# Who writes the order of three engines' queues: a scheduler or the program itself, in a two-layer attention and MLP kernel

## The chip, the core and the metric

The kernel runs on one core of one Trainium2 chip. The core has four engines that compute, each with a queue of its own that it works through in order: TensorE (PE in the profile, with PEld for the loading of its stationary operand), VectorE (DVE), ScalarE (ACT) and GpSimd (POOL). SyncE (SP) issues most of the DMAs here, ScalarE a few. Matmuls write PSUM, which has eight banks of 2 KB per partition; everything else lies in SBUF. The metric is the time of one execution on the device in microseconds, as the median of several runs.

## What is computed

Two layers of attention with a sliding window and an MLP, both with residuals and with the same weights in both layers. In short:

```
H, Dh, W = 32, 20, 256                       # S = 2048 rows, D = 640, F = 1536
def A(x):                                    # x already normalized
    q, k, v = split(x @ wqkv)                # heads of 20
    s = q k^T * Dh**-0.5, kept where 0 <= i - j < W
    return softmax(s) v @ wo
def B(x):
    h = relu(x @ w1 + b1)
    return (h * h) @ w2 + b2
for _ in range(2):
    x = x + A(layernorm(x))
    x = x + B(layernorm(x))
```

Input and output are float32. The dense products are made of three float16 products each, high by high, high by low and low by high part (`mm3`), so every operand of a dense matmul is written twice: a cast gives the high part, and a subtraction gives the low part.

## The kernel before

**Units.** The 2048 rows are cut into eight groups of 256 for each layer, so there are `NU = 16` units; unit `u` is group `u % 8` of layer `u // 8`. A unit's keys are its own 256 rows and those of the unit before. Weights stay in SBUF after the first 200 us or so, in which they are loaded and split.

**Attention of a unit.** `stage_qk` and `stage_v` make q, k and v with dense matmuls (line 155, as all of them). The two halves of q and k (tile `qd`: ScalarE writes the high part at L251, VectorE the low part at L252, from the PSUM tile `acc`) go out to DRAM and come back spread over partitions (`spread`). The 32 heads are worked in eight quads. For each quad there are three parts. `max_quad` makes the scores with rows as partitions (L321, 18 matmuls of a normal unit), and VectorE adds the mask and takes the row maximum in eight reductions (L335). `exp_quad` makes the scores again with keys as partitions (L371, 16 matmuls), with the maximum folded into the product as two more rows of `qt`; ScalarE takes six exponentials (L378), and GpSimd sets to zero what the window excludes, in eight instructions (L389, L393). `pv_quad` multiplies by V (L418, 32 matmuls in four columns of the array), with a column of ones that gives the sum of each row; ScalarE copies the result out (L428), and every second quad goes to DRAM.

**The rest of a unit.** `load_o` loads the attention's output and its row sums (`rs`) back, with the rows that the residual needs. `norm_o` divides: one reciprocal of all of `rs` (L464), two products (L467), two casts (L469) and two subtractions (L470), by halves of 128 columns. `stage_o` is the output projection with the residual (L482) and the second layer norm; `y_cross` and `ln_cross` cast and subtract the normalized rows (L220, L221) and transpose them by DMA (`cross`), while `stage_y` and `ln_t` transpose on TensorE. `stage_f` is the MLP: w1, then for each 128 hidden features relu (L517), square on GpSimd (L520), cast (L521) and subtraction (L522), then w2 and the residual (L534). `add_b2` adds the last bias on GpSimd (L492) to the residual rows.

**Order on TensorE.** It is the order of the program (`manual_schedule` for PE). `together` deals the eight quads of unit `u` out in turns: the exponential scores of one quad, a share of dense work, the maximum scores of a quad `LEAD = 5` quads ahead, pv, and dense work again. The dense work is a chain of generators: in a normal unit `stage_qk(u+1)`, `stage_o(u-1)`, `y_cross`, `stage_v(u+1)` and `stage_f(u-1)`.

**Order on the other engines.** It comes from the framework's scheduler, which replays the program on a timeline of its own and takes priorities: `first()` raises the priority of an instruction that reads a dense PSUM tile. The division of unit `u-1` is placed in the program by a `hook` in `stage_qk` (L242) between two tiles of k. The scheduler may move it.

**Buffers that tie engines together.** All dense products, pv and the small transposes share two PSUM banks (tag `mm`, `bufs=2`): a new tile waits until the tile two before it has been read. The scores share the other six (`bb`: three banks per half of the heads, `bufs=2`, taken in pairs), so the exponential scores wait for the reductions before them, and the maximum scores for the exponentials. The exponentials' output `pt` has six buffers, relu's output `r` two, `qd` one. `apart` declares that a matmul into one bank of `bb` doesn't depend on reads of the others, so that reads and matmuls of one quad may overlap.

Of the kernel before, what the change touches and what calls it, by code (L numbers as in the profile page):

```python
# [42 lines left out]
def kernel(ctx: ExitStack, tc: tile.TileContext, x, wqkv, wo, w1, b1, w2, b2, out):  # L43
# [47 lines left out]

    wq_s = sb.tile([P, 2, KC, 3 * D], F16, name="wq_s")
# [70 lines left out]
    def layernorm(src, y):  # L163

        st = sb.tile([P, 2, 6], F32, name="bst", bufs=2)
        for i in range(2):
            nc.vector.bn_stats(st[:, i, :], src[:, i * HD:(i + 1) * HD])
        mv = sb.tile([P, 4], F32, name="bmv", bufs=2)
        nc.vector.bn_aggr(mv[:, 0:2], st)
        nc.vector.tensor_scalar(mv[:, 2:3], mv[:, 1:2], 1e-5, YS ** -2, op0=ALU.add, op1=ALU.mult)  # L170
        power = nc.gpsimd.tensor_tensor(mv[:, 3:4], mv[:, 2:3], neghalf, op=ALU.pow)
        return nc.vector.tensor_scalar(y, src, mv[:, 0:1], mv[:, 3:4], op0=ALU.subtract, op1=ALU.mult), power

    def split_t(y, dst):

        for c0, n in ((0, 3), (3, 2)):
            tr = ps.tile([P, 4, P], F32, name="tr", tag="mm", bufs=2)
            for c in range(n):
                nc.tensor.transpose(tr[:, c, :], y[:, (c0 + c) * P:(c0 + c + 1) * P], ident)
            with first():  # L180
                nc.scalar.copy(dst[:, 0, c0:c0 + n], tr[:, :n])
                nc.vector.tensor_sub(dst[:, 1, c0:c0 + n], tr[:, :n], dst[:, 0, c0:c0 + n])  # L182
            yield 117 * n

# [11 lines left out]
    def ln_load(u):  # L196
# [3 lines left out]
        for i in range(2):  # L200
            xt = sb.tile([P, D], F32, name="xt", tag="xt", bufs=2)
            nc.sync.dma_start(xt, xsrc(l, 2 * g + i))
            did = layernorm(xt, xt)
            ys.append(xt)
            if u == 0:
                norm[:] = did
# [3 lines left out]
    def ln_t(u):  # L210
        ys = lns.pop(u)
        yTs[u] = yT = sb.tile([P, 2, KC, T], F16, name="yT", tag="yT", bufs=1)
        for i in range(2):
            yield from split_t(ys[i], yT[:, :, :, i * P:(i + 1) * P])

    def cross(ys, dst, tag):

        yl = sb.tile([P, 2, 2, D], F16, name="yl", tag=tag, bufs=1)
        for i, y in enumerate(ys):
            nc.scalar.copy(yl[:, i, 0], y)  # L220
            nc.vector.tensor_sub(yl[:, i, 1], y, yl[:, i, 0])  # L221
            for a in range(2):
                nc.sync.dma_start_transpose(dst[:, a, :, i * P:(i + 1) * P], yl[:, i, a])

    def ln_cross(u):

        ln_load(u)
        yTs[u] = sb.tile([P, 2, KC, T], F16, name="yT", tag="yT", bufs=1)
        cross(lns.pop(u), yTs[u], "qd")

    held = []

    def stage_qk(u, hold=False, hook=None):
# [4 lines left out]
        for j, dst in enumerate((qt, kt)):  # L238
            qd = sb.tile([P, KC, 2, T], F16, name="qd", tag="qd", bufs=1)
            for c0 in range(0, KC, 2):  # L240
                n = min(2, KC - c0)
                if hook and j and c0 == 2:  # L242
                    hook()
                acc = ps.tile([P, 2, T], F32, name="acc", tag="mm", bufs=2)
# [5 lines left out]
                with first():  # L250
                    at[0] = nc.scalar.activation(qd[:, c0:c0 + n, 0, :], acc[:, :n, :], AF.Copy, scale=s)  # L251
                    nc.vector.scalar_tensor_tensor(qd[:, c0:c0 + n, 1, :], acc[:, :n, :], s, qd[:, c0:c0 + n, 0, :],  # L252
                                                   op0=ALU.mult, op1=ALU.subtract)

            dr = tc.dram_tile([D, 3, T], F16, name=f"qk{u}_{j}")
            drv = dr.rearrange("(c p) t n -> p c t n", p=P)
            nc.sync.dma_start(drv[:, :, j:j + 2, :].rearrange("p c t n -> p c (t n)"),
                              qd.rearrange("p c a n -> p c (a n)"))
            nc.sync.dma_start(drv[:, :, 2 - 2 * j, :], qd[:, :, 0, :])
            if hold and j == 0:  # L260
                held.append((dst, dr))
            else:
                spread(dst, dr)
# [6 lines left out]
    def stage_v(u):  # L270
        yT = yTs.pop(u)
        for i in range(2):
            vt = vts[(2 * u + i) % 6][0]
            for h in range(2):
                acc = ps.tile([P, 2, T], F32, name="acc", tag="mm", bufs=2).rearrange("p a n -> p (a n)")
                yield from mm3(acc[:, :HD], lambda a, k: yT[:, a, k, i * P:(i + 1) * P],
                               lambda b, k: wq_s[:, b, k, 2 * D + h * HD:2 * D + (h + 1) * HD], KC, 136)
                with first():
                    at[0] = nc.scalar.activation(vt[:, h * NP:(h + 1) * NP, 0:DH],
                                                 acc[:, :HD].rearrange("p (h d) -> p h d", d=DH),  # L280
                                                 AF.Copy, scale=1.0 / (YS * WS))

# [3 lines left out]

    def banks():
        return [ps.tile([P, 3, 512], F32, name="bb", tag="bb", bufs=2) for e in range(2)]

    def apart(ins, others):  # L290

        for it in others:
            tc.declare_no_dep(ins.ins, it.ins, reason="other banks")

    def max_quad(n):
# [10 lines left out]

        found, read = [], []
        for w in (3, 0, 1, 2):
# [5 lines left out]
            o = parts[0][3]  # L314
            if w == 3:
                parts = [(kt, z, z + P, c + z - a) for kt, a, b, c in parts for z in range(a, b, P)]
            for kt, a, b, c in parts:
                for e in range(2):
                    r = slice(64 * e, 64 * e + 3 * DH)
                    to = bb[e][:, c // P, 3 * P:] if w == 3 else bb[e][:, w, c:c + b - a]  # L320
                    apart(nc.tensor.matmul(to, qt[r, p, i * P:(i + 1) * P], kt[r, p, a:b], start=True, stop=True),  # L321
                          read)
            now = []
            for e in range(2):
                s0 = p % (2 * GQ)
                accum = mx[:, e, s0, i:i + 1]
                if w == 3:
                    now.append((bb[e][:, o // P:, 3 * P:], maskb[:, o:].rearrange("p (a n) -> p a n", n=P), accum))
                else:
                    now.append((bb[e][:, w, o:3 * P], maskb[:, o:], accum))  # L330
            if w == 3:
                found = now
                continue
            for v, mask, accum in now + (found if w == 2 else []):
# [369 lines left out]
```

## Time and profile before

| | us |
|---|---|
| median of 3 runs | 1806.36 (1806.29 to 1808.37) |
| profiled execution | 1805.37 |
| its span, first to last instruction | 1803.6 |
| TensorE busy | 1632.8 (91% of the span) |
| VectorE busy | 975.7 (54%) |
| ScalarE busy | 760.7 (42%) |
| GpSimd busy | 631.2 (35%) |
| mean granted TensorE clock | 0.965 of full speed |

How to read the profile's lines: in a group of instructions, the line of the kernel, engine, operation, output<-input by the program's names, shapes and count come first; behind the first bar the busy time in us and the mean of one in ns; behind the second bar the time that the engine idled just before these instructions, and what ended that idle time. In a timeline, the first two numbers are start and duration in us, and the square bracket holds the idle time before and what ended it. In a table of stretches each row has the stretch, its length, the busy time of PE, PEld, DVE, ACT and POOL with their counts, the granted clock, the busy share of the DMA engines and GB/s.

### The profile page before, as it was taken

Reading aid. Unit: us, or ns where it says so; the run is one execution under the profiler, and the core shown is the slowest. Engines: PE = TensorE matmul, PEld = TensorE weight load, DVE = VectorE, ACT = ScalarE, POOL = GpSimd, SP = SyncE. Lnnn points to the kernel's source line nnn. Section 1 sums busy time; section 2 is a strip of 40 time slices with the busy share of each in tenths; the row PEclk is TensorE's granted clock in tenths of the full one; section 3 lists DMA queues with packets and bytes.
Section 4 is the critical chain, followed back from the end, with each engine's and each line's share of the span. In section 5 each row is a group of like instructions: output and inputs, shape, how many; then the busy total and the mean of one; then the engine's idle time right before and its main releaser. Section 6 shows DMA issues by size and latency. Waiting matters only on the chain. (4 is left out here: it accounts for less than half of the span.)

```text
span 1803.6 us, 44320 instructions
## 1 busy us (share of the span) xinstructions
PE 1632.8 (91%) x17542; PEld 1185.7 (66%) x17542; DVE 975.7 (54%) x3041; ACT 760.7 (42%) x1620; POOL 631.2 (35%) x1306
## 2 busy tenths in 40 slices
PE   4667699999999999999999999999999999898889
PEld 3444476766767676676777666676766767675567
DVE  6344555565565556556446565555656565555331
ACT  4355253533435343353534244353533435343522
POOL 4244152523425242342513243342423324242512
PEclk9888899999999999999999999999999999998999
DMA  5573303325152332515243342514234251331110
GB/s 180 143 189 97 96 10 106 79 71 133 39 132 54 100 85 71 133 35 132 58 121 71 97 100 71 129 34 126 55 89 111 60 126 46 95 73 38 35 54 20
DMA packets 230344, 157.42 MB, mean 87 GB/s; under 512 B 79608, under 2 KB 211064, under 8 KB 230136
## 3 DMA queue, kind: packets, MB, share of 16 engines
q1 hardware_dynamic: 221792, 145.08, 32.1%
q10 hardware_dynamic: 8344, 9.51, 1.8%
q8 instruction: 138, 2.26, 0.5%
q14 instruction: 70, 0.57, 0.1%
HBM read 84.68 MB, written 52.95 MB: 76 GB/s over the span
## 5 line engine op out<-in xcount | busy, mean ns | idle before, releaser
L335 DVE CUSTOM_DVE_ANT_0 bb<-bb,maskb 128x384 f32<-128x384 f32 (+2 forms) x1024 | 512.2, 563 | 129.3 <-PE bb L321 112.4
L378 ACT ACTIVATE pt<-bb 128x512 f32<-128x512 f32 x736 | 370.5, 603 | 224.5 <-PE bb L371 224.2
L389 POOL TENSOR_SCALAR_AFFINE_SELECT pt<-pt 128x256 f32<-128x256 f32 x448 | 186.2, 421 | 627.5 <-ACT pt L378 615.5
L155 PE MATMUL acc<-y,w_s 128*128 128x256 f16 x2880 | 333.5, 275 | 2.4 <-DVE y L182 2.2
L155 PE MATMUL acc<-w_s,hh 128*128 128x320 f16 x2304 | 327.6, 300 | 0.2
L155 PEld LDWEIGHTS <-w_s 128*128 128x128 f16 x2880 | 278.5, 99 | 59.1 <-issue 24.0
L155 PE MATMUL acc<-yT,wq_s 128*128 128x256 f16 x2400 | 296.4, 285 | 9.7 <-DVE qd L252 5.3
L155 PEld LDWEIGHTS <-hh 128*128 128x128 f16 x2304 | 222.4, 98 | 99.0 <-issue 15.9
L155 PEld LDWEIGHTS <-wq_s 128*128 128x128 f16 x2400 | 239.0, 102 | 69.5 <-issue 33.5
L418 PE MATMUL pv<-pt,vt 128*32 128x128 f32 (+1 forms) x3840 | 204.5, 344 | 56.3 <-DVE qd L252 36.6
L393 POOL TENSOR_SCALAR_AFFINE_SELECT pt<-pt 128x256 f32<-128x256 f32 x512 | 206.8, 427 | 60.3 <-ACT pt L378 59.3
L428 ACT COPY ot<-pv 128x256 f32<-128x256 f32 x128 | 47.5, 371 | 376.4 <-PE pv L418 376.4
L418 PEld LDWEIGHTS pv<-pt,vt 128*32 128x32 f32 x3840 | 111.3, 113 | 110.0 <-issue 61.3
L522 DVE TENSOR_TENSOR hh<-r,hh 128x256 f16<-128x256 f32 x192 | 84.2, 449 | 181.1 <-ACT hh L521 174.8
L155 PE MATMUL acc<-wo_s,od 128*128 128x320 f16 x960 | 141.3, 301 | 25.1 <-ACT od L469 9.8
L520 POOL TENSOR_TENSOR r<-r 128x256 f32<-128x256 f32 x192 | 116.5, 627 | 130.7 <-ACT r L517 130.7
L155 PE MATMUL acc<-wq_s,yT 128*128 128x320 f16 x960 | 142.1, 301 | 6.3 <-DVE qd L252 3.3
L335 DVE DVE_READ_ACCUMULATOR2_ANT mx<- 128x1 f32 x1024 | 145.0, 142 | 0.0
L155 PEld LDWEIGHTS <-od 128*128 128x128 f16 x960 | 91.7, 98 | 72.1 <-issue 27.2
L252 DVE SCALAR_TENSOR_TENSOR qd<-acc,qd 128x512 f16<-128x512 f32 (+1 forms) x96 | 56.4, 598 | 140.9 <-ACT qd L251 140.9
L371 PE MATMUL bb<-qt,kt 62*128 62x128 f16 (+1 forms) x1920 | 110.8, 246 | 22.5 <-DVE mx L335 18.0
L155 PEld LDWEIGHTS <-yT 128*128 128x128 f16 x960 | 93.1, 99 | 50.4 <-issue 15.5
(63 smaller groups left out, 1150.0 us busy)
## 6 DMA issues: line engine op xcount, KB each, us to landing
qk<-qd SPq DMA_DIRECT2D x32, 640.0 KB
qt<-qk SPq DMA_DIRECT2D x32, 480.0 KB
kt<-qk SPq DMA_DIRECT2D x32, 480.0 KB
o<-ot SPq DMA_DIRECT2D x256, 42.0 KB
qk<-qd SPq DMA_DIRECT2D x32, 320.0 KB
od<-o SPq DMA_DIRECT2D x14, 640.0 KB
stg<-in_B_w_dram ACTq DMA_DIRECT2D x30, 256.0 KB
xt<-in_A_x_dram SPq DMA_DIRECT2D x16, 320.0 KB
```

The lines of the kernel that those rows point to most:

```text
L155: nc.tensor.matmul(acc, lhs(a, c), rhs(b, c), start=(k == 0), stop=(k == 3 * nk - 1))
L252: nc.vector.scalar_tensor_tensor(qd[:, c0:c0 + n, 1, :], acc[:, :n, :], s, qd[:, c0:c0 + n, 0, :], op0=ALU.mult, op1=ALU.subtract)
L335: read.append(nc.vector.tensor_tensor_reduce(out=v, in0=v, in1=mask, scale=1.0, scalar=-3.0e38, op0=ALU.add, op1=ALU.max, accum_out=accum))
L371: apart(nc.tensor.matmul(bb[e][:, k, o:o + w], kt[r, 2 * qd + j, ko:ko + P], qt[r, 2 * qd + j, q0 * P:q0 * P + w], start=True, stop=True), ...
L378: at[0] = nc.scalar.activation(pt[:, :o], bb[e][:, k, :o], AF.Exp, scale=SCALE / (QS * QS))
L389: nc.gpsimd.affine_select(out=m, in_=m, pattern=[[0, 2], [-1, P]], compare_op=ALU.is_gt, fill=0.0, base=0, channel_multiplier=1)
L393: nc.gpsimd.affine_select(out=m, in_=m, pattern=[[0, 2], [1, P]], compare_op=ALU.is_ge, fill=0.0, base=0, channel_multiplier=-1)
L418: nc.tensor.matmul(pv[32 * jj:32 * (jj + 1), q0 * P:(q0 + qn) * P], vf[:, c:c + 32], pj[:, j, :], start=(k == 0), stop=(k == len(steps) - ...
L428: nc.scalar.copy(ot[:, qd % 2], pv)
L520: nc.gpsimd.tensor_tensor(r, r, r, op=ALU.mult)
L522: nc.vector.tensor_sub(hh[:, 1, f0 + f, :], r, hh[:, 0, f0 + f, :])
```

## The change

ScalarE, VectorE and GpSimd get the order of the program from unit 1 on (`manual_schedule` for the three). So that the program's order is a useful one, the instructions are no longer written where they arise, but posted as jobs. A job has an engine, a cost in ns, a function that writes the instruction, jobs it depends on, an earliest time and a priority (0 for what frees a PSUM tile of the dense work, 1 for exponentials, masks and reductions, 2 for what has time). A small clock runs along with the program: every piece of dense work adds its ns (`step`), each score and pv block a constant, and after each step `pump` puts down the jobs whose start on their engine's clock is no more than 250 ns ahead. `need` puts a job down at once, with what it depends on, where TensorE's next instruction needs it. Units before 1 put each job down at once and leave the order to the scheduler as before.

The following goes with it:

- The division is posted by `load_o` itself in four quarters of 64 columns, each a reciprocal, a product, a cast and a subtraction, with an earliest time 7 us later; `norm_o` and the hook are gone. The first layer norm and `add_b2` get earliest times of 4 us, and `add_b2` is cut into four halves of 320 columns.
- In `max_quad` all 18 matmuls are written before the eight reductions, and in `exp_quad` all 16 before the six exponentials. `apart` is gone.
- `y_cross` and `ln_cross` post their casts and subtractions; DMAs that follow a job are issued when the job is put down.
- TensorE's instructions stand in the same order, but for four matmuls near the end (`upto(dense, 10e3)` in place of 6e3 and 4e3).

The core of the diff:

```diff
+    now, clk, pend, ordered = [0.0], {"A": 0.0, "D": 0.0, "G": 0.0}, [], [False]
+    LOOK, LAT = 250.0, 80.0
+    class Job:
+        def __init__(self, eng, cost, fn, deps, nb, prio):
...
+        def start(self):
+            return max([clk[self.eng], self.nb] + [d.end + LAT for d in self.deps])
+        def put(self):
+            t = self.start()
+            self.out = self.fn()
+            self.end = clk[self.eng] = t + self.cost
+    def post(eng, cost, fn, *deps, wait=0.0, prio=1):
+        j = Job(eng, cost, fn, [d for d in deps if d is not None], now[0] + wait, prio)
+        if ordered[0]:
+            k = len(pend)
+            while k and pend[k - 1].prio > prio:
+                k -= 1
+            pend.insert(k, j)
...
+    def pump():
...
+            for j in pend:
+                if all(d.end is not None for d in j.deps) and j.start() <= now[0] + LOOK:
+                    pend.remove(j)
+                    j.put()
...
+    def need(*js):
+        for j in js:
+            if j.end is None:
+                need(*j.deps)
+                pend.remove(j)
+                j.put()
+            now[0] = max(now[0], j.end)
+    def step(ns):
+        now[0] += ns
+        pump()
+    def mm_tile(shape, name):
+        while len(banks2) > 1:
+            need(*banks2.pop(0))
+        t = ps.tile(shape, F32, name=name, tag="mm", bufs=2)
+        banks2.append([])
+        return t, banks2[-1]
...
     def stage_qk(u, hold=False):
-                if hook and j and c0 == 2:
-                    hook()
+                lo_ = post("D", 60 + 265 * n, low, post("A", 60 + 225 * n, high, prio=0), prio=0)
+                jobs.append(lo_)
+            need_later(lo_, lambda j=j, dst=dst, qd=qd: leave(u, j, dst, qd, hold))
...
     def banks():
+        need(*bbjobs)
+        bbjobs.clear()
         return [ps.tile([P, 3, 512], F32, name="bb", tag="bb", bufs=2) for e in range(2)]
...
+                bbjobs.append(post("D", 115 + 1.04 * (3 * P - o), lambda v=v, mask=mask, accum=accum:
+                                   nc.vector.tensor_tensor_reduce(...)))
...
+                ex = post("A", 30 + 0.9 * o, power)
+                bbjobs.append(ex)
...
+                    masks.append(post("G", 410, mask, ex))
...
     def load_o(u, late=False):
+        for i in range(4):
+            q = slice(i * T // 4, (i + 1) * T // 4)
...
+            j = post("D", 460, ratio, wait=7e3, prio=2)
+            j = post("D", 400, times, j, prio=2)
+            j = post("A", 350, high, j, prio=2)
+            js.append(post("D", 400, low, j, prio=2))
-    def norm_o(u):
...
     def add_b2(u, *after):
+            for h in range(2):
+                js.append(post("G", 870, lambda x1=x1s[u, i], hs=hs:
+                               nc.gpsimd.tensor_tensor(x1[:, hs], x1[:, hs], box["b"][:, hs], op=ALU.add),
+                               wait=4e3, prio=2))
...
     def stage_f(u, ahead=None):
+                j = post("A", 380, relu, *hj[f0 + f - 2:f0 + f - 1], prio=0)
+                jobs.append(j)
+                j = post("G", 630, square, j, prio=0)
+                j = post("A", 330, high, j, prio=0)
+                hj.append(post("D", 430, low, j, prio=0))
...
+        if u == 1:
+            ctx.enter_context(tc.manual_schedule(engines={mybir.EngineType.Activation, mybir.EngineType.DVE,
+                                                          mybir.EngineType.Pool}))
+            ordered[0] = True
```

351 lines of the change are left out of this document (219 added, 132 removed).

## The prediction

> **What bounds the kernel now.** I read the page first, then the busy time by stage, then the idle time of TensorE by what ended it, and last one unit in order of time. A unit is 256 rows of one layer, some 105 us; it has eight turns, each with the scores of one quad for the exponential (tile bb, L371), the scores of a later quad for the row maximum (bb, L321), the product with V (pv, L418), and dense matmuls (L155) between.
>
> ```profile
> PE 1632.8 (91%) x17542; PEld 1185.7 (66%) x17542; DVE 975.7 (54%) x3041; ACT 760.7 (42%) x1620; POOL 631.2 (35%) x1306
> 0.00:200.00 200.00, 127.60 (x1051) 87.01 (x1051) 91.02 (x324) 93.37 (x194) 76.21 (x106) 0.86 0.57 156
> 200.00:300.00 100.00, 91.09 (x1043) 63.74 (x1044) 58.95 (x187) 42.70 (x91) 35.55 (x80) 0.94 0.11 33
> 300.00:1600.00 1300.00, 1235.15 (x13660) 905.66 (x13659) 751.16 (x2323) 551.39 (x1171) 451.81 (x979) 0.98 0.37 89
> ```
>
> TensorE is the bound. Its instruction order is the same in the changed kernel but for four matmuls of the tail, so only its idle time and its clock can move. Of 170.8 us idle, 72.4 lie in the first 200 us, where the order hardly changes. From 300 to 1600 us it idles 64.9 us. Who ends that idle time, in the groups by line of this stretch:
>
> ```profile
> L418 PE MATMUL pv<-pt,vt 128*32 128x256 f32 (+1 forms) x3040 | 160.0, 345 | 48.4 <-DVE qd L252 33.9 <-POOL pt L393 11.2 <-ACT r L517 3.3
> L155 PE MATMUL acc<-wo_s,od 128*128 128x320 f16 x780 | 112.7, 299 | 9.7 <-DVE qd L252 9.7
> L371 PE MATMUL bb<-qt,kt 62*128 62x256 f16 (+1 forms) x1536 | 85.7, 244 | 5.8 <-DVE bmv L169 2.5 <-DVE mx L335 1.5 <-DVE bmv L170 1.4
> ```
>
> Three quarters of it hangs on one instruction, VectorE's low half of qd (L252), because pv needs the PSUM bank that it frees. One unit on VectorE and TensorE shows why it is late:
>
> ```profile
> 394.93 1.75 DVE L464 RECIPROCAL rs<-rs 128x256 f32<-128x256 f32 x1 [3.09 <-DMA rs<-o]
> 397.00 1.56 DVE L467 TENSOR_TENSOR od<-od,rs 128x640 f32<-128x640 f32 x2 [0.32 <-DMA od<-o]
> 398.62 1.56 DVE L470 TENSOR_TENSOR od<-od 128x640 f16<-128x640 f32 x2
> 400.10 0.68 DVE L252 SCALAR_TENSOR_TENSOR qd<-acc,qd 128x512 f16<-128x512 f32 x1
> 400.93 2.79 PE L418 MATMUL pv<-pt,vt 128*32 128x256 f32 x32 [2.51 <-DVE qd L252]
> 407.72 0.83 PE L371 MATMUL bb<-qt,kt 62*128 62x256 f16 x16
> 414.27 1.51 PE L418 MATMUL pv<-pt,vt 128*32 128x256 f32 x32
> 418.87 2.20 PE L155 MATMUL acc<-wo_s,od 128*128 128x320 f16 x15 [0.81 <-DVE qd L252]
> 442.86 0.99 PE L418 MATMUL pv<-pt,vt 128*32 128x256 f32 x8 [1.76 <-POOL pt L393]
> 456.23 4.00 PE L155 MATMUL acc<-y,w_s 128*128 128x256 f16 x35
> ```
>
> VectorE stands 3.09 us at the reciprocal for a DMA, does the whole division, and only then qd; TensorE idles 2.51 us. The gap also costs clock: the same 32 pv matmuls take 2.79 us behind it and 1.51 us at 414.27. The stretches of these two, with the granted clock as third from last:
>
> ```profile
> 400.93:403.70 2.77, 2.77 (x33) 1.56 (x34) 2.77 (x11) 0.00 (x0) 0.00 (x0) 0.50 0.00 0
> 414.27:415.78 1.51, 1.51 (x37) 0.93 (x34) 1.51 (x7) 0.00 (x0) 0.00 (x0) 1.00 1.08 217
> ```
>
> **The change, part by part.** *Division in quarters, 7 us after its load (load_o).* In the built order the eight maximum reductions and qd's low half now stand ahead of the first quarter. The maximum scores of this turn end at 398.4 (400.93 less the wait), the reductions 4.2 us later (below), so the first quarter comes no sooner than 402.6, when the DMA of 394.93 has long landed. Both waits go: -33.9 us, and -2.28 for the same wait at 295.04 (below).
>
> ```profile
> 295.04 2.79 PE L418 MATMUL pv<-pt,vt 128*32 128x256 f32 x32 [2.28 <-DVE qd L252]
> 1552.80 2.79 PE L418 MATMUL pv<-pt,vt 128*32 128x256 f32 x32 [4.10 <-DVE qd L252]
> 1650.26 1.75 DVE L464 RECIPROCAL rs<-rs 128x256 f32<-128x256 f32 x1 [7.97 <-DMA rs<-o]
> 1648.43 2.35 PE L155 MATMUL acc<-w_s,hh 128*128 128x320 f16 x16
> 1658.90 1.95 PE L371 MATMUL bb<-qt,kt 62*128 62x256 f16 x16 [8.12 <-DVE mx L335]
> ```
>
> The clock: eight such pv, these two the first and the last of them, at 2.79 for 1.51: 8 x 1.28 = 10.2 us; the other units' gaps cool less or not at all. With the exponential scores at 1658.90 (1.95 for 0.83) I take -11.3 us.
> The Trainium skill, "TensorE: Matmul & The Clock Gate", Part 1, says that the clock drops after at least one idle window of about 3.4 us. By that a gap of 2.5 us costs no clock, and of this term only the two gaps over 3.4 us (4.10 and 8.12) would remain, 2.4 us; the trace disagrees (clock 0.50 behind 2.51 us).
>
> *The last unit's division* (1650.26): VectorE no longer stands 7.97 us ahead of the reductions. What is late next: in that turn 4.2 us of reductions and a residual add of half a microsecond against pv's 1.44 and the 2.35 us at 1648.43 (1 us); a turn later the reductions share VectorE with two subtractions of the division (1.56 / 4 each) and another add, 5.5 us against the same 3.8 (2 us). -8.1 + 3 = -5.1.
>
> *What quarters cost.* Per unit VectorE issues 12 instructions for 5, ScalarE 4 for 2. A fixed part per instruction follows from two sizes of one operation:
>
> ```profile
> L335 DVE CUSTOM_DVE_ANT_0 bb<-bb,maskb 128x384 f32<-128x384 f32 x732 | 384.3, 589 | 80.4 <-PE bb L321 79.4
> L335 DVE CUSTOM_DVE_ANT_0 bb<-bb,maskb 128x128 f32<-128x128 f32 x32 | 9.1, 313 | 6.5 <-PE bb L321 6.5
> ```
>
> 589 - 313 = 276 ns for 256 columns leaves 175 ns at none: 7 x 0.175 = 1.2 us a unit, which VectorE's idle 42% of this stretch hides; I take nothing. With that cover gone it is 1.2 x 15 = 18 us.
>
> *qd at the output projection* (418.87, 0.81 us): the low half now goes ahead of the last three reductions. -9.7, of which I take 9.
>
> *Masks* (442.86): x + b2 on GpSimd stood ahead of two masks:
>
> ```profile
> 439.40 3.04 POOL L492 TENSOR_TENSOR x<-x,xt 128x640 f32<-128x640 f32 x2 [2.19 <-DMA qt<-mT]
> ```
>
> It becomes four halves of about 0.8 us, behind the squares, where six masks have a whole turn. -10 of 11.2. Their 3.04 us hide in GpSimd's 65% idle time.
>
> *What is added.* (1) Ahead of qd's last low half stand now a quarter reciprocal and product, about 0.44 + 0.4 us, by the rows above divided by four. Behind it on SP is the store qk<-qd, behind that ScalarE's next qd, behind that the next pv:
>
> ```profile
> 407.15 0.42 DVE L252 SCALAR_TENSOR_TENSOR qd<-acc,qd 128x256 f16<-128x256 f32 x1 [0.73 <-ACT qd L251]
> 407.60 0.48 SPq L257 DMA_DIRECT2D qk<-qd  x1
> 412.36 0.60 ACT L251 ACTIVATE qd<-acc 128x512 f16<-128x512 f32 x1 [1.11 <-DMA qk<-qd]
> 412.99 0.69 DVE L252 SCALAR_TENSOR_TENSOR qd<-acc,qd 128x512 f16<-128x512 f32 x1 [5.41 <-ACT qd L251]
> 414.04 0.57 DVE L335 CUSTOM_DVE_ANT_0 bb<-bb,maskb 128x384 f32<-128x384 f32 x1 [0.37 <-PE bb L321]
> 418.13 0.14 DVE L335 DVE_READ_ACCUMULATOR2_ANT mx<- 128x1 f32 x1
> 408.20 3.04 ACT L378 ACTIVATE pt<-bb 128x512 f32<-128x512 f32 x6 [1.09 <-PE bb L371]
> 447.80 0.84 ACT L517 ACTIVATE r<-acc,b1s 128x256 f32<-128x256 f32 x2 [2.97 <-PE acc L155]
> ```
>
> Before, qd is free at 413.68 and pv starts at 414.27: 0.59 us of slack. The low half ends about 1.05 us later against the scores: 0.46 us of new wait, x 12 units = +5.5.
> (2) Without the declared independence of the banks, the reductions start when all 18 score matmuls are done, and the exponentials when all 16 are (0.83 us after 407.72, not 0.48). First row to last they take 4.2 us (414.04 to 418.27); from the maximum's end to the next scores TensorE has 1.44 us of pv and 35 matmuls of 4.0: 5.4 us. With qd's 0.69 between them 4.9 to 5.1 us: hidden by 0.3 to 0.5 us.
> (3) In the first dense layer, relus and casts of hh stand ahead of the last exponentials on ScalarE. Worst turn: six exponentials 3.04, four relus 2 x 0.84, two casts 0.8, together 5.5 us, against the 5.1 us of 45 matmuls before the maximum scores, which need all six. +0.5 x 13 = +6.5, while the old 3.3 us for r goes: +3.2.
> (4) The second yl cast comes behind six exponentials and a V copy, so its transposes on SP land about when the first dense layer starts: between 0 and 0.5 us a unit; half of it, +3.
> (5) In unit 1 VectorE subtracts the transposed y ahead of the reductions, so the next scores wait some 2.5 us, 1 us of it won before: +1.5.
> (6) Four places where the sum above leaves under 0.3 us (qd at 0.2, the projection 0.3, mT 0.1, the hh cast ahead of the sixth turn's reductions 0.25). Bounds: nothing, or 0.3 us at each, 16 us in all. Those slacks are sums of means, so I take half a microsecond a unit: +7.
> (7) The 5.8 us of bb stay. The tail's o -> od chain starts a quarter earlier: -2.
>
> *Sum*: -33.9 - 2.3 - 11.3 - 5.1 - 9 - 10 + 5.5 + 3.2 + 3 + 1.5 + 7 - 2 = -53.4 us. The profiled execution took 1805.37 us (span 1803.6), 1.0 under the median of 1806.36; so 1752 on its scale, 1753 on the median's. Both sides: with the added terms at nothing and bb's waits gone -33.9 - 2.3 - 11.3 - 8.1 - 9.7 - 11.2 - 3.3 - 5.8 - 3 = -89, 1718; with the added 5.5 + 6.5 + 3 + 1.5 + 7 doubled -30, 1776.
>
> **The rivals.** *The waits move more than they go.* At five places a unit the slack is half a microsecond or less; if each lacks 0.5 us, 5 x 0.5 x 13 = 32 us in place of term 6: -53 - 7 + 32 = -28, 1778. For it: queues run in order, and a planner that is off by 0.5 us is enough. Against it: the old order met the same turns with 1.5 us of such waits in 1300.
>
> *Slower: exponentials stuck behind relus.* r has two buffers, so a relu waits for the square, cast and subtraction of the one two before:
>
> ```profile
> L517 ACT ACTIVATE r<-acc,b1s 128x256 f32<-128x256 f32 x192 | 84.5, 484 | 95.3 <-PE acc L155 93.3
> L520 POOL TENSOR_TENSOR r<-r 128x256 f32<-128x256 f32 x192 | 116.5, 627 | 130.7 <-ACT r L517 130.7
> L521 ACT CAST hh<-r 128x256 f16<-128x256 f32 x192 | 76.9, 408 | 52.9 <-POOL r L520 52.9
> L522 DVE TENSOR_TENSOR hh<-r,hh 128x256 f16<-128x256 f32 x192 | 84.2, 449 | 181.1 <-ACT hh L521 174.8
> ```
>
> That ring is 0.48 + 0.63 + 0.41 + 0.45 = 1.97 us over three engines. In the new order exponentials stand behind such a relu in the three turns of the first layer, and the maximum scores behind the sixth. If the ring shows whole in each, 3 x 1.97 x 13 = 77 us: 1753 + 77 = 1830, slower. It decides from 1.4 us a turn. Against it: the relus' tiles finish 3.4 us apart (30 matmuls at the 4.00/35 above), longer than the ring.
>
> *Gaps without clock*: by the mechanism that only gaps over 3.4 us cool, the clock term falls from 11.3 to 2.4 and the time is 1761. The page named above states it; the trace speaks against it.
>
> *No change in the order* is excluded: built, the division stands behind the reductions.
>
> **How the numbers follow.** Forecast 1753 (1725 to 1770): 0.60. Moved waits, 1770 to 1795: 0.20. Clock kept, 1761, inside the first's range: 0.02. More gone than I count, under 1722: 0.03. Within 0.2% (3.6 us, about what a measurement can tell here): 0.03. Slower: 0.12, the ring or a like one. The range 1722 to 1795 leaves out 0.03 below and some 0.15 above. Faster 0.85, same 0.03, slower 0.12.
>
> **What would show it.** Right: no wait of pv for qd, granted clock 1.00 from 300 to 1600 us, TensorE busy near 1620 us, its idle time there near 35 us, division behind the reductions. Step 1 shows as pv waiting for qd once a unit by half a microsecond, step 3 as maximum scores waiting for an exponential, step 4 as a wait for y<-yl. The prediction is wrong if the scores L371 wait for the reductions in most turns, or if the relus of the first layer idle with exponentials behind them.

## The result and the profile after

The changed kernel takes 1742.72 us (median of 4 runs, 1741.30 to 1744.47) against 1806.51 us (1806.29 to 1808.37) for the kernel before: a ratio of 0.9645, 95% interval 0.9628 to 0.9662. The profiled execution took 1741.30 us, with a span of 1739.6; it is compared with the 1805.37 and 1803.6 of before. The forecast was 1753, range 1722 to 1795.

Engines on the page of the changed kernel, and below them its longest stage (columns as before: stretch, length, busy time of PE, PEld, DVE, ACT, POOL, granted clock, DMA share, GB/s):

```profile
PE 1612.3 (93%) x17542; PEld 1177.3 (68%) x17542; DVE 989.7 (57%) x3153; ACT 761.4 (44%) x1652; POOL 666.2 (38%) x1338
```

```profile
300.00:1600.00 1300.00, 1273.59 (x14381) 940.09 (x14378) 802.17 (x2544) 583.47 (x1267) 510.12 (x1066) 1.00 0.37 91
```

The 64.0 us of span split into 43.5 us of TensorE's idle time (170.8 to 127.3) and 20.5 us of its busy time (1632.8 to 1612.3, for the same 17542 matmuls). From 300 to 1600 us the clock went from 0.98 to 1.00 and the idle time from 64.9 to 26.4 us; the stretch now holds 14381 matmuls in place of 13660. What is left there, by group:

```profile
L223 PE MATMUL acc<-y,w_s 128*128 128x256 f16 x2340 | 270.0, 274 | 8.5 <-DMA y<-yl 7.9 <-ACT ot L570 0.5
L558 PE MATMUL pv<-pt,vt 128*32 128x256 f32 (+1 forms) x3236 | 154.0, 330 | 4.0 <-DVE qd L356 4.0
L223 PE MATMUL acc<-wq_s,yT 128*128 128x320 f16 x780 | 114.4, 299 | 4.3 <-DVE mT L468 4.3
L223 PE MATMUL acc<-wo_s,od 128*128 128x320 f16 x785 | 113.6, 299 | 2.4 <-DVE od L625 1.2 <-DVE qd L356 1.0
L438 PE MATMUL bb<-kt,qt 60*128 60x128 f16 (+1 forms) x1826 | 89.2, 234 | 5.9 <-ACT pt L510 5.7
L497 PE MATMUL bb<-qt,kt 62*128 62x128 f16 (+1 forms) x1616 | 86.0, 244 | 1.0 <-DVE mx L450 1.0
```

The pv row answers to the first of before: 33.9 us for qd became 4.0, and the masks and r are gone from it. New are the waits for y<-yl, for mT and of the maximum scores for an exponential. The turn that stood at 400.93 us before, from the timeline after:

```profile
396.36 0.69 DVE L356 SCALAR_TENSOR_TENSOR qd<-acc,qd 128x512 f16<-128x512 f32 x1 [4.28 <-ACT qd L353]
398.57 1.51 PE L558 MATMUL pv<-pt,vt 128*32 128x256 f32 x32
401.94 0.69 DVE L356 SCALAR_TENSOR_TENSOR qd<-acc,qd 128x512 f16<-128x512 f32 x1
403.54 0.55 DVE L615 RECIPROCAL rs<-rs 128x64 f32<-128x64 f32 x1
409.46 0.60 ACT L353 ACTIVATE qd<-acc 128x512 f16<-128x512 f32 x1 [1.91 <-DMA qk<-qd]
409.95 0.59 ACT L510 ACTIVATE pt<-bb 128x512 f32<-128x512 f32 x1
410.60 0.82 PE L438 MATMUL bb<-kt,qt 60*128 60x128 f16 x17 [0.65 <-ACT pt L510]
```

The first low half of qd now stands ahead of the division, pv starts without a wait and runs at full clock (1.51 us), and the reciprocal has no wait, since its DMA has landed. The last three lines are a price: ScalarE stands 1.91 us at the high half of the next qd, until the store of the qd before it has landed (qd has one buffer), and the last exponential, which the maximum scores need, stands behind it. It is the pattern of the division again, on another engine. ScalarE stands there in every unit from 300 to 1600 us, mostly for 0.8 us, which costs TensorE nothing.

### The profile page after: what moved, and what is told of

Same layout as the page of the kernel before. It is cut to its first block, busy times and chain, and to the rows that moved or that the text cites. A ratio compares the mean times of both kernels' runs of the same rounds, so it can differ in the third digit from the quotient of the medians.

```text
span 1739.6 us, 44188 instructions
## 1 busy us (share of the span) xinstructions
PE 1612.3 (93%) x17542; PEld 1177.3 (68%) x17542; DVE 989.7 (57%) x3153; ACT 761.4 (44%) x1652; POOL 666.2 (38%) x1338
## 4 chain that ended last, share of the span: by engine, by line
PE 66%; DVE 10%; DMA 5%; ACT 5%; issue 3%; POOL 3%; SPq 0%; ACTq 0%; DVEq 0%; POOLq 0%
PE acc L223 49%; PE pv L558 7%; DVE bb L450 5%; PE bb L497 5%; PE bb L438 5%; ACT pt L510 3%; DMA qk<-qd 2%; DMA y<-yl 2%; POOL r L707 1%; DMA rs<-o 1%; POOL bmv L249 1%; DVE mx L450 1%; ACT r L703 1%; DVE od L625 1%; POOL pt L525 1%
## 5 line engine op out<-in xcount | busy, mean ns | idle before, releaser
L510 ACT ACTIVATE pt<-bb 128x512 f32<-128x512 f32 x736 | 377.7, 600 | 196.0 <-PE bb L497 195.4
L525 POOL TENSOR_SCALAR_AFFINE_SELECT pt<-pt 128x256 f32<-128x256 f32 x448 | 203.5, 461 | 567.8 <-ACT pt L510 554.9
L223 PE MATMUL acc<-yT,wq_s 128*128 128x256 f16 x2400 | 287.9, 280 | 9.5 <-DVE qd L356 5.1
L223 PEld LDWEIGHTS <-wq_s 128*128 128x128 f16 x2400 | 234.7, 100 | 62.2 <-issue 29.5
L529 POOL TENSOR_SCALAR_AFFINE_SELECT pt<-pt 128x256 f32<-128x256 f32 x512 | 210.5, 433 | 70.6 <-ACT pt L510 69.7
L713 DVE TENSOR_TENSOR hh<-r,hh 128x256 f16<-128x256 f32 x192 | 89.5, 471 | 244.4 <-ACT hh L710 234.7
L558 PE MATMUL pv<-pt,vt 128*32 128x128 f32 (+1 forms) x3840 | 189.3, 331 | 7.4 <-DVE qd L356 4.5
L558 PEld LDWEIGHTS pv<-pt,vt 128*32 128x32 f32 x3840 | 104.4, 110 | 54.7 <-issue 21.3
L703 ACT ACTIVATE r<-acc,b1s 128x256 f32<-128x256 f32 x192 | 81.3, 480 | 93.6 <-PE acc L223 91.2
```

Source lines behind the costliest of these rows:

```text
L223: nc.tensor.matmul(acc, lhs(a, c), rhs(b, c), start=(k == 0), stop=(k == 3 * nk - 1))
L510: at[0] = nc.scalar.activation(box["pt"][:, :o], bb[e][:, k, :o], AF.Exp, scale=SCALE / (QS * QS))
L525: nc.gpsimd.affine_select(out=m, in_=m, pattern=[[0, 2], [-1, P]], compare_op=ALU.is_gt, fill=0.0, base=0, channel_multiplier=1)
L529: nc.gpsimd.affine_select(out=m, in_=m, pattern=[[0, 2], [1, P]], compare_op=ALU.is_ge, fill=0.0, base=0, channel_multiplier=-1)
L558: nc.tensor.matmul(pv[32 * jj:32 * (jj + 1), q0 * P:(q0 + qn) * P], vf[:, c:c + 32], pj[:, j, :], start=(k == 0), stop=(k == len(steps) - ...
L703: nc.scalar.activation(box["r"], acc[:, f, :], AF.Relu, bias=b1s[:, f0 + f:f0 + f + 1], scale=1.0 / (YS * WS))
```

## The experiments

In these runs the kernel before took 1802.2 to 1802.5 us, so kernels are compared by their ratio to it; 0.9645 is the changed kernel, and 0.001 is 1.8 us. The changed kernel was not run again beside them, so this takes it that both kernels shift alike from session to session, which no run shows: between the profiled executions most differences from the changed kernel are smaller, by up to 7 us.

| run | us | ratio (95%) |
|---|---|---|
| division moved alone, in the kernel before | 1755.04 | 0.9742 (0.9723 to 0.9762) |
| no earliest time for the division | 1819.49 | 1.0096 (1.0076 to 1.0116) |
| division in one piece | 1761.99 | 0.9772 (0.9754 to 0.9791) |
| order on VectorE only | 1768.88 | 0.9819 (0.9801 to 0.9836) |
| transposes urgent | 1736.55 | 0.9633 (0.9617 to 0.9649) |
| relus behind exponentials | 1820.43 | 1.0098 (1.0077 to 1.0119) |
| costs at zero | 2074.97 | 1.1514 (1.1494 to 1.1534) |
| one priority | 1868.73 | 1.0363 (1.0344 to 1.0381) |
| bias added whole | 1746.53 | 0.9692 (0.9674 to 0.9711) |
| power's cost, bias load later | 1744.43 | 0.9691 (0.9673 to 0.9709) |
| the same, casts urgent | 1756.49 | 0.9748 (0.9731 to 0.9766) |
| the same, norm urgent | 1767.42 | 0.9805 (0.9786 to 0.9823) |

### The division moved alone, in the kernel before

```diff
-                if hook and j and c0 == 2:
+                if hook and j and c0 == 0:
...
-        nc.vector.reciprocal(rs, rs)
+        with behind(low[0]): nc.vector.reciprocal(rs, rs)    # low[0]: the last L252 of q
```

The other place of the hook and the tie belong together: no run here has the one without the other.

> The kernel before with one thing moved: the reciprocal is tied behind VectorE's low half of the last q tile (L252), so that the undivided division stands behind the eight reductions; TensorE, GpSimd and SyncE keep their order. Theory (the gain is the place of the division): the waits of pv for qd go (36.6 us of idle time) and TensorE's busy time falls by 13 to 20 us with its clock; the masks (15 us), r (3.3), the 9.7 at the output projection and the last unit's 8 stay. 1753 to 1760 us. Rival (what counts is the program's order on all three engines, and a division moved alone only hands the wait to the next qd or to the reductions behind 5 us of division): 1775 us or more, with a new wait of 1.5 to 2 us in each unit.

The theory's range held, 1755.04 us. Engines and the group of pv over the whole span in this run:

```profile
PE 1615.7 (92%) x17542; PEld 1176.7 (67%) x17542; DVE 978.6 (56%) x3041; ACT 758.3 (43%) x1620; POOL 662.0 (38%) x1306
```

```profile
L418 PE MATMUL pv<-pt,vt 128*32 128x128 f32 (+1 forms) x3840 | 193.2, 330 | 19.0 <-POOL pt L393 11.0 <-ACT r L517 3.2 <-DVE qd L252 2.5
```

The wait for qd fell from 36.6 to 2.5 us, and with it TensorE's busy time by 17.1 us, while the masks (11.0 of 15.0 us), r (3.2) and the output projection (9.5) kept most of their waits. The rival's new wait of 1.5 to 2 us in each unit did not come. The division's place is thus worth 47 of the 64 us (2.58 of 3.55%), with neither quarters nor a planner.

### No earliest time for the division

```diff
-            j = post("D", 460, ratio, wait=7e3, prio=2)
+            j = post("D", 460, ratio, prio=2)
```

> The changed kernel without the 7 us that the division waits behind its load; all else is as in the changed kernel. The quarters then stand ahead of the first low half of qd, as in the kernel before. Theory (VectorE stands at the reciprocal for the DMA, and the planner's order is worth nothing there without the 7 us): pv waits for qd again, 2 to 2.5 us in each of 13 units, and the clock falls behind these gaps: +28 to +33 us of idle time, +10 to +20 us of busy time, 1780 to 1796 us. Rival (the order of the engines and the cut into quarters carry the gain): below 1760 us.

The mechanism is the theory's, but larger: 1819.49 us, 1.0% slower than the kernel before. Timeline of one turn and the group of pv from 300 to 1600 us:

```profile
405.00 0.55 DVE L615 RECIPROCAL rs<-rs 128x64 f32<-128x64 f32 x1 [5.54 <-DMA rs<-o]
406.75 0.49 DVE L618 TENSOR_TENSOR od<-od,rs 128x320 f32<-128x320 f32 x1 [1.19 <-DMA od<-o]
410.34 0.68 DVE L356 SCALAR_TENSOR_TENSOR qd<-acc,qd 128x512 f16<-128x512 f32 x1
411.17 2.79 PE L558 MATMUL pv<-pt,vt 128*32 128x256 f32 x32 [5.13 <-DVE qd L356]
```

```profile
L558 PE MATMUL pv<-pt,vt 128*32 128x256 f32 (+1 forms) x3072 | 154.1, 342 | 51.6 <-DVE qd L356 51.6
```

VectorE stands for the row sums and then for `od`, 6.7 us here against 3.41 before, so the gaps of these 13 units are 2.9 to 5.1 us where I had put 2 to 2.5. The same written order costs 81 us more without this one earliest time; cut and order gain nothing without it.

### The division in one piece

```diff
-        for i in range(4):
-            q = slice(i * T // 4, (i + 1) * T // 4)
+        for i in range(1):
+            q = slice(0, T)                # costs 1750, 1600, 1400, 1600
```

> The changed kernel with the division in one piece (one reciprocal, product, cast and subtraction over 256 columns) at the same earliest time. Theory (the place counts, the cut little): the third low half of q stands behind a reciprocal of 1.75 us in place of 0.55 + 0.49, and the first of k behind a product of 1.6 us; 0 to 0.7 us a unit, 1743 to 1752 us. Rival (the quarters are what let qd through): 1765 us or more, with pv waiting for qd over 1.5 us in each unit.

1761.99 us: neither theory. pv waits for qd no more than in the changed kernel (4.2 us). The price is elsewhere, as VectorE's timeline in one unit and the group of the projection from 300 to 1600 us show:

```profile
512.80 1.49 DVE L625 TENSOR_TENSOR od<-od 128x1280 f16<-128x1280 f32 x1 [0.94 <-ACT od L622]
518.86 0.42 DVE L356 SCALAR_TENSOR_TENSOR qd<-acc,qd 128x256 f16<-128x256 f32 x1
```

```profile
L223 PE MATMUL acc<-wo_s,od 128*128 128x320 f16 x780 | 112.7, 299 | 8.0 <-DVE qd L356 8.0
```

Reductions and qd stand behind an undivided subtraction, the last low half of k ends half a microsecond later, and the output projection waits 0.72 us for it in 11 units (0.25 in the changed kernel, where it waits). In unit 1 and the tail the projection waits for a whole cast in place of a quarter (waits for od of 16.7 us over the whole span, 11.6 in the changed kernel). The quarters gain about 23 us by the ratios (16 between the profiled executions), of which these rows show 7 + 5; next to none comes through pv, and where the rest lies stays open.

### The order on VectorE only

```diff
-            ctx.enter_context(tc.manual_schedule(engines={mybir.EngineType.Activation, mybir.EngineType.DVE,
-                                                          mybir.EngineType.Pool}))
+            ctx.enter_context(tc.manual_schedule(engines={mybir.EngineType.DVE}))
```

> The changed kernel with only VectorE in the program's order; ScalarE and GpSimd are left to the scheduler. Theory (the gain sits on VectorE): the waits for qd stay away, and 5 to 20 us come back as waits for masks and r (15 and 3.3 us before) and as exponentials and relus in another order; 1740 to 1763 us. Rival (the three orders only work together): 1775 us or more.

1768.88 us, 31 us above the changed kernel by ratio: between the two, nearer the rival. Two groups from 300 to 1600 us, and one place in order of time:

```profile
L558 PE MATMUL pv<-pt,vt 128*32 128x256 f32 (+1 forms) x3168 | 158.3, 331 | 24.9 <-POOL pt L529 11.2 <-ACT r L703 8.1 <-DVE qd L356 5.6
L223 PE MATMUL acc<-wq_s,yT 128*128 128x320 f16 x780 | 116.1, 299 | 16.8 <-ACT vt L398 14.6 <-DVE mT L468 1.4
```

```profile
537.66 0.72 ACT L310 CAST yl<-xt 128x640 f16<-128x640 f32 x1 [2.17 <-DVE xt L251]
538.29 3.03 ACT L510 ACTIVATE pt<-bb 128x512 f32<-128x512 f32 x6
541.16 0.81 ACT L398 ACTIVATE vt<-acc 128x320 f32<-128x320 f32 x2
541.70 1.79 PE L223 MATMUL acc<-wq_s,yT 128*128 128x320 f16 x12 [1.32 <-ACT vt L398]
```

The masks (11.2) and r (8.1) are the waits I had named. The 14.6 us for V I had not: ScalarE stands 2.17 us at a cast for VectorE, then takes all six exponentials, and only then the copy of V that frees the PSUM bank. With an order for VectorE alone, such a stand came up on another engine here.

### Transposes urgent

```diff
-            j = post("A", 700, high, ready, *js[-1:], prio=2)
-            js.append(post("D", 900, low, j, prio=2))
+            j = post("A", 700, high, ready, *js[-1:], prio=0)
+            js.append(post("D", 900, low, j, prio=0))
```

> The changed kernel with the casts and subtractions of the normalized rows (L310, L314) at priority 0 in place of 2. Theory (step 4 of the prediction, mis-sized: the second cast stands behind six exponentials, and the low half of mT behind a normalization that waits for GpSimd): the waits of TensorE for y<-yl (7.9 us) and for mT (4.3 us) go, so 8 to 12 us less than the changed kernel, a ratio of 0.958 to 0.961 to the kernel before. Rival (a cast of 0.75 us ahead of the last exponential only moves the wait to the maximum scores, twice a unit): a ratio of 0.968 or more, with maximum scores waiting for an exponential some 0.5 us in those turns.

0.9633: the fastest run, but its interval overlaps that of the changed kernel, and it lies between theory and rival. The wait for mT went (4.3 to 0.3 us), that for y<-yl hardly (groups from 300 to 1600 us):

```profile
L223 PE MATMUL acc<-y,w_s 128*128 128x256 f16 x2340 | 270.1, 274 | 7.8 <-DMA y<-yl 6.6 <-ACT ot L570 0.5 <-ACT vt L398 0.5
L223 PE MATMUL acc<-wq_s,yT 128*128 128x320 f16 x780 | 112.6, 299 | 0.3 <-DVE mT L468 0.3
```

### Relus behind exponentials

```diff
-                j = post("A", 380, relu, *hj[f0 + f - 2:f0 + f - 1], prio=0)
+                j = post("A", 380, relu, *hj[f0 + f - 2:f0 + f - 1], prio=1)
...
-                j = post("A", 330, high, j, prio=0)
+                j = post("A", 330, high, j, prio=1)
```

> The changed kernel with the relus and casts of the first dense layer at the priority of the exponentials, so that they stand behind those that were posted before them. Theory (step 3): the maximum scores' waits for the last exponential in the first dense layer go (0.27 us in 11 units, and about 2 us in unit 1: 5 us), and waits of pv for r come back (3.3 us in the kernel before, 8.1 with the scheduler's order on ScalarE): -2 to +4 us, a ratio of 0.963 to 0.967. Rival (the relus' two buffers and the two banks of PSUM need them early): a ratio of 0.972 or more.

1820.43 us, 82 us above the changed kernel by ratio: the rival's side, by a mechanism that neither had. One turn in order of time, and the group of the exponential scores:

```profile
464.41 0.82 DVE L713 TENSOR_TENSOR hh<-r,hh 128x256 f16<-128x256 f32 x1 [2.21 <-ACT hh L710]
465.15 0.55 DVE L450 CUSTOM_DVE_ANT_0 bb<-bb,maskb 128x384 f32<-128x384 f32 x1
...
466.66 0.41 DVE L713 TENSOR_TENSOR hh<-r,hh 128x256 f16<-128x256 f32 x1
...
469.50 0.27 PE L497 MATMUL bb<-qt,kt 62*128 62x256 f16 x1 [1.97 <-DVE mx L450]
```

```profile
L497 PE MATMUL bb<-qt,kt 62*128 62x256 f16 (+1 forms) x1520 | 88.2, 248 | 43.6 <-DVE mx L450 43.5
```

With the casts later on ScalarE, VectorE stands 2.21 us at a subtraction of hh that needs such a cast, with the reductions behind it and more subtractions among them, and the exponential scores wait for the reductions, 1.6 to 2.0 us twice a unit (43.5 us). TensorE's busy time rises by 29 us with it. The maximum scores' waits that I wanted to remove fell from 5.7 to 2.2 us.

### Costs at zero, and one priority

```diff
-        j = Job(eng, cost, fn, [d for d in deps if d is not None], now[0] + wait, prio)
+        j = Job(eng, 0.0 if ordered[0] else cost, fn, [d for d in deps if d is not None], now[0] + wait, prio)
```

> The changed kernel with the cost of every job taken as zero from unit 1 on, so that the planner's clock only knows when inputs are ready and not how long an engine is taken; priorities and earliest times stay. Theory (measured times matter because reductions and exponentials that are put down all at once shut out a qd that comes half a microsecond later): pv and the projection wait for qd again, 1 to 3 us in two or three places of each unit: +25 to +80 us, 1765 to 1820 us. Rival (priorities and earliest times do the work, the costs add little): within 10 us of the changed kernel, a ratio below 0.971.

2074.97 us: the theory's direction, but 337 us above the changed kernel by ratio, four times the most I had given it. The other run removes urgency:

```diff
-            while k and pend[k - 1].prio > prio:
-                k -= 1
             pend.insert(k, j)
```

> The changed kernel with one priority for all jobs from unit 1 on: costs and earliest times stay, but among jobs that are ready, the one posted first goes first. Theory (urgency matters less than the costs, because a qd is posted when only a few reductions are left, and the 7 us keep the division behind them): +5 to +30 us, a ratio of 0.967 to 0.981. Rival (without urgency qd stands behind all that is ready, as in the kernel before): a ratio of 0.985 or more.

1868.73 us: the rival. Groups of the run without costs, and below them the turn of the run with one priority:

```profile
L223 PE MATMUL acc<-yT,wq_s 128*128 128x256 f16 x1644 | 203.0, 284 | 94.8 <-DVE qd L356 94.8
L558 PE MATMUL pv<-pt,vt 128*32 128x256 f32 (+1 forms) x2560 | 135.0, 354 | 86.4 <-ACT r L703 45.4 <-DVE x L737 38.2 <-DVE x L644 2.9
```

```profile
418.51 0.55 DVE L615 RECIPROCAL rs<-rs 128x64 f32<-128x64 f32 x1
419.50 0.56 DVE L450 CUSTOM_DVE_ANT_0 bb<-bb,maskb 128x384 f32<-128x384 f32 x1
423.26 1.95 PE L497 MATMUL bb<-qt,kt 62*128 62x256 f16 x16 [5.12 <-DVE mx L450]
```

Without costs the planner puts all of the division down at once, and qd behind it: 8.7 us in one place of each unit. The second row shows that pv waits for r and for the residual adds (x) as well; what puts these late I did not trace. With one priority the division, ready first, goes ahead of the reductions, and the exponential scores wait 5.12 us. A written order gains here only with all three: earliest time, costs and urgency.

### The bias added whole

```diff
-            for h in range(2):
-                hs = slice(h * HD, (h + 1) * HD)
-                js.append(post("G", 870, ...[:, hs]..., wait=4e3, prio=2))
+            js.append(post("G", 1600, lambda x1=x1s[u, i]:
+                           nc.gpsimd.tensor_tensor(x1, x1, box["b"], op=ALU.add), prio=2))
```

> The changed kernel with x + b2 in two whole additions and no earliest time, as posted before the first squares: on GpSimd they now stand behind the masks of their turn and ahead of the first squares. Theory (what cost 11 us in the kernel before was that the additions stood ahead of masks; the cut into halves and the 4 us are not needed for that): within 4 us of the changed kernel, a ratio of 0.9625 to 0.967. Rival (two additions of 1.5 us, and the DMA of b2 that they wait for, hold up squares, and with them r and pv): 1 us or more in each unit, a ratio of 0.9715 or more.

1746.53 us, 0.9692 (0.9674 to 0.9711): a little above the theory's 0.967 and below the rival's 0.9715. From 300 to 1600 us neither the masks nor r are among what pv waits for (its 4.0 us are all qd), and TensorE idles 27.9 us there against 26.4. So the order behind the masks ends the 11 us. By the ratios the cut and the earliest time together add some 8 us, and the two intervals lie apart; between the profiled executions it is 2.8 us (1744.10 against 1741.30). I found no place for them.

### Three attempts at what is left

The first raises the planner's cost of the power (to the 1.07 us that one of them took) and moves the load of b2; the second adds priority 0 for `y_cross`; the third also for the second layer norm:

```diff
-        power = j = post("G", 600, ...
+        power = j = post("G", 1100, ...
...
+            with behind(trl[0] if ordered[0] else None): nc.sync.dma_start(box["b"], ...   # trl[0]: last transpose
```

> The changed kernel with two corrections: the planner's cost of GpSimd's power (L249) 1100 ns in place of 600, by the measured 1.07 us, and the load of b2 (L658) behind the second pair of transposes on SyncE in place of ahead of it. Theory (the planner puts the normalization ahead of mT because it takes the power for shorter than it is; the second transposes are late by what stands before them on SyncE, not by priority): the wait for mT goes (4.3 us to 0.5), that for y<-yl falls by half (7.9 to 4): 5 to 9 us less, a ratio of 0.9595 to 0.962. Rival (both waits are set by the DMA's flight alone): 0.9635 to 0.9655.

> As the run with the power's cost and the load of b2 corrected, and with the casts and subtractions of y_cross at priority 0 (those of ln_cross stay at 2). Theory: the second transposes leave another 0.5 to 1 us earlier, y<-yl waits 0 to 3 us in all; a ratio of 0.958 to 0.961. Rival (the cast ahead of the last exponential costs what it brings): the same ratio as without it, to 0.001.

> As the run before, and with the second layer norm's statistics, power and normalization at priority 0 too, so that all four transposes stand ahead of mT's DMAs on SyncE. Theory: y<-yl waits for nothing any more, but the exponential scores wait for reductions that now stand behind statistics (0.9 us in one turn of each unit, against some 0.5 us of slack): 0 to +6 us against the run without it. Rival (the slack holds): 1 to 3 us less than without it.

Each is slower than the changed kernel: 0.9691, 0.9748, 0.9805. The first two are above both theory and rival; the third costs 10 us against the second, where the theory gave 0 to 6. Lines of the first (SyncE's queue, the first normalization, y), of the second (y) and of the third (scores), and the last two powers of one unit in the changed kernel:

```profile
528.73 0.61 DVE L251 TENSOR_SCALAR xt<-x,bmv 128x640 f32<-128x640 f32 x1
530.20 2.56 SPq L316 DMA_TRANSPOSE y<-yl  x2
532.86 3.46 SPq L473 DMA_DIRECT2D qt<-mT  x4
536.41 2.55 SPq L316 DMA_TRANSPOSE y<-yl  x2
```

```profile
L223 PE MATMUL acc<-y,w_s 128*128 128x256 f16 x2340 | 268.9, 273 | 18.4 <-DMA y<-yl 17.2 <-ACT vt L398 0.6 <-ACT ot L570 0.5
```

```profile
L223 PE MATMUL acc<-y,w_s 128*128 128x256 f16 x2340 | 275.6, 277 | 23.1 <-DMA y<-yl 22.5 <-ACT ot L570 0.5
```

```profile
L497 PE MATMUL bb<-qt,kt 62*128 62x256 f16 (+1 forms) x1584 | 89.2, 248 | 23.5 <-DVE mx L450 23.5
```

```profile
521.40 0.55 POOL L249 TENSOR_TENSOR bmv<-bmv,neghalf 128x1 f32<-128x1 f32 x1
528.89 1.07 POOL L249 TENSOR_TENSOR bmv<-bmv,neghalf 128x1 f32<-128x1 f32 x1 [6.95 <-DVE bmv L243]
```

The new cost was not truer. In the changed kernel's trace the power takes 1.07 us in one place of a unit, the second half of the second layer norm, and 0.55 us in the median of its 64 executions; ahead of the first normalization it takes 0.55. With 1100 ns there the planner puts the first normalization behind the reductions, and the first transposes leave 2.2 us later, counted from the projection's first residual add (L644). mT now comes ahead of the second normalization (its wait falls to 0.3 us). In both kernels SyncE's queue runs almost without a break from the first transposes over mT's four issues to the second transposes; these now start 0.1 to 1.3 us later, while the first dense layer could start earlier by what mT no longer costs, and y<-yl waits 17.2 us in place of 7.9. The run changes cost and load at once; their shares are not separated.

In the second, the second normalization stands 3.18 us for its power on GpSimd, and the second transposes start 18.5 us behind that residual add in every normal unit, where the first had 17.5 in seven of eleven; y<-yl waits 22.5 us. The third ends that wait altogether and hands 23.5 us to the exponential scores, whose last reduction now stands behind statistics and normalization.

## Why the prediction was right, and where not

The forecast's idle time was right almost to the microsecond, and its clock was not: -42.1 against -43.5 us idle, -11.3 against -20.5 us busy. The first is luck in part. The main term came as forecast, but others missed by 2 to 5 us each and cancelled: y (4.7 us worse than forecast), the tail and the last unit against the scores' old waits, the tight places and the masks.

*qd* (-33.9 - 2.3 + 5.5 = -30.7): 36.6 became 4.5 us over the whole span, -32.1. Step (1), the store behind the late low half, came in six units and not once in each by half a microsecond: in two units pv waits for qd (1.43 and 2.57, the 4.0 us), and in four the last exponential stands behind the high half of qd and the maximum scores wait, 2.6 us in all. That is 6.6 us, near the 5.5, but in part at a place that the step did not have. The prediction says that three quarters of the idle time from 300 to 1600 us hang on the low half of qd; its rows give 33.9 + 9.7 of 64.9, two thirds.

*Clock* (-11.3): the term that failed. "The other units' gaps cool less or not at all" is wrong: three of those five cool, only later, and two of the eight that I counted stay cold longer than pv. In the kernel before, by stretch (pv, then the 35 dense matmuls behind it, of 4.00 us when warm):

```profile
403.70:407.70 4.00, 4.00 (x38) 3.35 (x35) 2.33 (x8) 1.35 (x3) 0.00 (x0) 0.96 0.00 0
1341.35:1342.94 1.59, 1.59 (x33) 0.98 (x34) 1.59 (x7) 0.00 (x0) 0.00 (x0) 0.91 0.00 0
1342.94:1348.40 5.46, 5.46 (x37) 4.11 (x39) 3.51 (x12) 1.35 (x3) 0.00 (x0) 0.71 0.02 3
```

Behind the gap of 2.35 us at 1341.35 pv ran at 0.91 and looked warm, but the dense matmuls behind it took 5.46 us. If the clock is either half or full, half clock lasted 2 x 0.09 x 1.59 + 2 x 0.29 x 5.46 = 3.5 us there, and 2.77 + 2 x 0.04 x 4.00 = 3.1 us behind the gap at 400.93. Worked out in the same way it is 2.9 to 3.5 us behind nine of the eleven gaps that cool, and 5.6 and 4.9 us behind those at 719.23 and 1552.80. Counting pv alone I missed the five dense groups of 5.03 to 5.54 us. The division moved alone shows the net price of these gaps, 17.1 us. The Trainium skill, "TensorE: Matmul & The Clock Gate", Part 1, has a window of some 3.4 us that runs freely; the half clock behind nine gaps is near its length, that behind the other two is not. That a whole idle window is needed doesn't agree: gaps of 2.2 to 2.6 us did it.

*The last unit* (-5.1): the 8.12 us went; in its place come 4.48 us of transposes waiting for the normalization and 1.21 at the projection. From the matmuls ahead of that gap to the next w1, TensorE idles 8.8 us in place of 12.1: -3.3. The tail's -2 did not come: its wait ahead of the projection was 2.23 and is 2.19 us.

*qd at the projection* (-9): 9.7 became 1.0. *Masks* (-10): 15.0 became 2.3 over the span, -12.7.

*(3) Relus* (+6.5 - 3.3): the waits came, at 0.27 us in 11 units and 1.9 us in unit 1, 4.9 in all, and r's 3.3 went; half a microsecond a unit was double. The slower rival, exponentials behind relus, did not come; the reverse order costs 82 us.

*(4) Transposes* (+3): 7.7, more than double. *(5) Unit 1* (+1.5): its transposes wait 3.61 us in place of 2.61, and the waits behind them are about as before; not foreseen, the matmuls behind run cold (5.26 us for 4.00). *(6) Four tight places* (+7): mT has 4.0, the other three nearly none. *(7)* bb's 5.8 us were to stay; 1.0 is left.

Of the rivals, the moved waits are refuted as a sum (26.4 us of idle time from 300 to 1600 us, where they need 35 - 7 + 32 = 60; by the prediction's own terms the 35 should be 31), though some of my own edits did just that. The clock by gaps over 3.4 us alone is refuted by the 17.1 us.

## What to carry to other kernels

Look on every engine for an instruction that stands at a transfer while what the bound engine needs waits behind it; moving that one instruction behind another took three quarters of this gain, and the changed kernel has such a stand left on ScalarE. A written order is only as good as its earliest times, costs and priorities. Where the places were within half a microsecond, a new priority or cost of one item moved the wait to the next item: try one at a time and read who waits then. Take a cost from the median of all executions at its place, not from one row. Price a clock drop over all matmuls behind a gap, not over the first group.

## What was not expected of the hardware

How long a gap is doesn't decide by itself whether the clock falls. In the run without an earliest time three gaps of 2.92, 3.37 and 2.86 us left pv at 1.51 us and the dense group at 4.17 to 4.18 (granted clock 1.00); in the kernel before gaps of 2.28 and 2.40 us had pv at 2.79. All five gaps of 4.1 us and more ahead of pv in the two traces left it cold. Two of the warm lines:

```profile
1023.66 1.51 PE L558 MATMUL pv<-pt,vt 128*32 128x256 f32 x32 [2.86 <-DVE qd L356]
1025.10 4.18 PE L223 MATMUL acc<-yT,wq_s 128*128 128x256 f16 x35
```

The four issues of mT's DMAs hold SyncE's queue for about 2.4 to 3.5 us and a pair of transposes for 2.5 to 4.0 us (the changed kernel and the run with the power's cost), so that, back to back, they set when the second transposes leave.
